# Moving four heads of an output projection from the 512-column pass to the 128-column tail of a decode attention kernel

## The chip, the core and the metric

The kernel runs on one core of a Trainium2 chip. The metric is device time in microseconds of one execution; the time before is the median of three runs.

## The reference, cut to what matters

For two batch rows of 512 values (`B, D = 2, 512`), with 32 query heads, 8 key and value heads, a cache of 32768 positions and heads of 128 values:

```python
xn = _layernorm(x, axis=-1)
q = (xn @ wq)                                # 32 heads of 128
scores = einsum("bhqd,bhkd->bhqk", q, k) * (Dh ** -0.5)
p = _softmax(scores, axis=-1)
o = einsum("bhqk,bhkd->bhqd", p, v)
s = o.reshape(B, Sq, Hq * Dh) @ wo           # (4096, 512)
h = relu(xn @ w1 + b1) ** 2
g = _silu(h @ w2 + b2)
return x + s * g
```

The caches are 512 MB of float32, read once. `wo` is 8 MB: 32 heads of 128x512 float32, 256 KB each.

## The kernel before, in words

One pair of batch row and key/value head is cut in two halves of 16384 positions, so there are `NT = 32` steps. In each, `kslot` receives 8 MB of keys and `vslot` 8 MB of values, both single buffers; TensorE multiplies the four queries of the group with the keys (`pe_scores`), a softmax piece is formed on VectorE and ScalarE, and TensorE multiplies the probabilities with the values (`pe_values`). Each engine runs its own loop; the order between them is set by semaphores alone. SP issues all large loads on one queue, each as soon as its buffer is free. Three prologue turns (`PRO = 3`) go through the same `pe_values` code with other contents in `vslot` and `pT`: the two matrices of the gate and `wq`.

`pe_values` (line 357) is 32 products. Product `n` takes 16 columns of `pT` as weights and 512 columns of `vslot` as the moving operand, and adds into `o_ps`, into the quarter of its partitions that `n % 4` names. Ahead of products 8, 16, 24 and 28 it waits for the semaphores `ge`, `gb`, `gc` and `gd`. In the loop these were given their counts beforehand, or are given them by loads.

After the 32 steps comes the product with `wo`, over the 32 heads of both rows, in three kinds:

- Heads 0 to 11 (`NX`, the first piece): their weights are in `wbuf`, their attention outputs in `oX`, and `pe_extra` (line 392) adds 12 wide products into `wb`.
- The further pieces of 8, 4 and 4 heads: SP loads them into `vslot` at places 8 to 15, 24 to 27 and 28 to 31 (semaphores `ge`, `gc`, `gd`), VectorE writes the heads' outputs to the same places of `pT` (`turned`, lines 405 and 406), and one more turn of `pe_values` adds them into `o_ps`. The other 16 places of `pT` are set to zero (line 407), so their products run over zeros.
- The last four heads (`TOP`), in pieces of 2, 1 and 1 (`TAIL`): their weights go to `wbuf` behind the first twelve, their outputs to `oN`. Each head takes four products (line 422), one for each block of 128 columns of `wo`, into the four quarters of partitions of `acc`. So `acc` holds 128 columns where `o_ps` holds 512.

The wide sums are brought to the shape of `acc` by a fold: VectorE adds `wb` and `o_ps` in two halves into `o_sb` (line 415; `t_w` names the two), and four products with the selection matrix `selg` (line 426) add the four blocks of 128 columns into `acc`. TensorE runs its instructions in program order, so the place of the fold among the narrow heads is written out: `if h == TOP - 2`, behind the third of four. Last, VectorE multiplies `acc` with the gate, adds `x`, and SP stores 64 KB (lines 430 to 434).

SP's last block (line 324) issues the loads of `wo`: the first at once, the piece of eight when product 15 of the last step is done (`vh`), all others when the last step's `pe_values` is done.

## Time and profile before

| | |
|---|---|
| runs before, median of 3 | 1302.14 us (1302.06 to 1302.2) |
| span of the profiled execution | 1300.8 us |
| its own time | not listed apart from the span; the median is 1.3 us above it |
| busy in the span: TensorE products, weight loads, VectorE, ScalarE, GpSimd | 53%, 15%, 7%, 8%, 0% |
| moved | 561 MB, 431 GB/s |

The profile is of one execution, times are from its start. A float32 product is two instructions (passes), each with its own weight load; products on different quarters of the partitions run beside each other, so several times of one instruction overlap. A busy share of TensorE is therefore no share of its peak. "PEld" is TensorE's weight load, "SPq" a transfer's issue by SP.

### The profile page before, as it was taken

What the parts mean: (1) busy time and instruction counts of PE and PEld (TensorE: products, weight loads), DVE (VectorE), ACT (ScalarE), POOL (GpSimd) and SP (SyncE); (2) the same over time, 40 slices, a digit from 0 to 9 for tenths busy, and PEclk for the clock granted to TensorE, in tenths of its full rate; (3) what the DMA queues carried; (4) which work ended last, traced back from release to release, by engine and by line L of the source; (5) the groups of instructions that cost most, each with busy time, mean ns of one, the idle gap of its engine ahead of it and who ended that gap; (6) DMA issues with size and microseconds to landing.
All of it is one profiled execution on the core that took longest, in us unless ns stands there. A gap on an engine that the chain in (4) does not pass through costs nothing.

```text
span 1300.8 us, 11201 instructions
## 1 busy us (share of the span) xinstructions
PE 691.4 (53%) x4781; PEld 189.5 (15%) x4781; DVE 86.0 (7%) x366; ACT 99.1 (8%) x202; POOL 5.7 (0%) x22
## 2 busy tenths in 40 slices
PE   3746546545545545645544644654554554554557
PEld 0111111111111111111111111111111111111112
DVE  2100000000000000000000000000000000000001
ACT  0301001010010001001010100001001000100100
POOL 1000000000000000000000000000000000000000
PEclk9877677677778677767767767767767767776878
DMA  9999999999999999999999999999999999999998
GB/s 420 419 451 419 447 423 429 441 419 451 419 451 419 451 419 431 439 419 451 419 451 419 451 419 431 439 419 451 419 451 419 451 419 431 439 419 451 419 435 373
DMA packets 10840, 561.08 MB, mean 431 GB/s; under 512 B 1216, under 2 KB 1368, under 8 KB 1752
## 3 DMA queue, kind: packets, MB, share of 16 engines
q1 hardware_dynamic: 10800, 561.06, 99.8%
q10 hardware_dynamic: 40, 0.02, 0.0%
HBM read 561.01 MB, written 0.07 MB: 431 GB/s over the span
## 4 chain that ended last, share of the span: by engine, by line
DMA 74%; PE 24%; issue 1%; DVE 0%; POOL 0%; SPq 0%; POOLq 0%
DMA vslot<-in_vt 70%; PE o_ps L364 24%; DMA wbuf<-in_wo 3%; DMA vslot<-in_wm 1%; PE wb L392 0%; DVE vslot L209 0%; DVE vslot L206 0%; PE acc L422 0%; POOL pT L197 0%; POOL pT L179 0%; SPq L243 0%; PE acc L426 0%; SPq L242 0%; DVE yb L430 0%; DVE xb L432 0%
## 5 line engine op out<-in xcount | busy, mean ns | idle before, releaser
L364 PE MATMUL o_ps<-vslot,pT 128*16 128x512 f32 x2304 | 327.6, 732 | 225.7 <-DMA vslot<-in_vt 201.5
L347 PE MATMUL sc<-kslot,qz 128*32 128x512 f32 x2048 | 294.1, 739 | 277.1 <-DMA kslot<-in_kt 277.1
L347 PEld LDWEIGHTS sc<-kslot,qz 128*32 128x32 f32 x2048 | 71.2, 132 | 478.5 <-DMA kslot<-in_kt 284.7
L364 PEld LDWEIGHTS o_ps<-vslot,pT 128*16 128x16 f32 x2304 | 69.6, 112 | 454.6 <-issue 223.5
L309 ACT ACTIVATE prob<-sc,nm 128x512 f32<-128x512 f32 x32 | 22.0, 687 | 633.9 <-DVE nm L277 633.9
L270 DVE TENSOR_REDUCE r<-sc 128x1 f32<-128x512 f32 x32 | 22.1, 692 | 557.7 <-PE sc L347 557.7
L318 ACT COPY o_sb<-o_ps 128x512 f32<-128x512 f32 x32 | 18.8, 586 | 480.2 <-PE o_ps L364 480.2
L353 PE MATMUL tp<-ident,prob 128*128 128x128 f32 x128 | 25.6, 333 | 50.7 <-ACT prob L309 50.7
L291 DVE TENSOR_REDUCE t<-ot 128x4 f32<-128x64 f32 x32 | 7.2, 225 | 547.6 <-PE ot L374 547.6
L374 PE MATMUL ot<-ident,o_sb 128*128 128x128 f32 x140 | 23.0, 287 | 25.0 <-ACT o_sb L318 22.9
L353 PEld LDWEIGHTS tp<-ident,prob 128*128 128x128 f32 x128 | 16.4, 164 | 56.8 <-ACT prob L309 56.8
L350 PE MATMUL ms<-ident,r 128*128 128x128 f32 x32 | 10.3, 323 | 26.4 <-DVE r L270 26.4
L374 PEld LDWEIGHTS ot<-ident,o_sb 128*128 128x128 f32 x140 | 14.7, 140 | 57.3 <-ACT o_sb L318 52.4
L311 ACT COPY pT<-tp 128x512 f32<-128x512 f32 x32 | 18.8, 586 | 28.4 <-PE tp L353 28.4
L309 ACT ACT_TABLE_LOAD x16 | 20.5, 1283 | 0.3
L350 PEld LDWEIGHTS ms<-ident,r 128*128 128x128 f32 x32 | 4.2, 133 | 55.4 <-DVE r L270 55.4
L355 PEld LDWEIGHTS ms<-selh,l 128*128 128x128 f32 x64 | 12.1, 236 | 0.0
L355 PE MATMUL ms<-selh,l 128*128 128x4 f32 x64 | 10.5, 235 | 0.0
L273 DVE TENSOR_REDUCE mh<-ms 128x4 f32<-128x128 f32 x32 | 9.3, 292 | 10.9 <-PE ms L350 10.9
L200 ACT COPY vslot<-wbuf 128x4096 f32<-128x4096 f32 x2 | 7.1, 3610 | 0.0
L309 ACT ACTIVATION_READ_ACCUMULATOR prob<-sc,nm 128x1 f32 x32 | 6.2, 192 | 0.0
L392 PE MATMUL wb<-wbuf,oX 128*16 128x512 f32 x24 | 4.4, 900 | 2.2 <-DMA wbuf<-in_wo 2.2
(86 smaller groups left out, 78.0 us busy)
## 6 DMA issues: line engine op xcount, KB each, us to landing
vslot<-in_vt SPq DMA_DIRECT2D x2, 4096.0 KB, 24.0
vslot<-in_wm SPq DMA_DIRECT2D x1, 7168.0 KB, 19.4
wbuf<-in_wo SPq DMA_DIRECT2D x1, 3072.0 KB, 34.9
vslot<-in_wo SPq DMA_DIRECT2D x1, 2048.0 KB, 13.6
vslot<-in_wo SPq DMA_DIRECT2D x2, 1024.0 KB, 12.0
kslot<-in_kt SPq DMA_DIRECT2D x32, 29.4
wbuf<-in_wo SPq DMA_DIRECT2D x1, 512.0 KB, 13.9
wbuf<-in_wo SPq DMA_DIRECT2D x2, 256.0 KB, 14.2
```

The source lines that it names most:

```text
L270: v.tensor_reduce(r1[:, :], sc[:, :], axis=AX.X, op=ALU.max).then_inc(dm, 1)
L273: did(f"mh{u}", v.tensor_reduce(mh[:, u, :], ms[:, :P].rearrange("p (a h) -> p h a", h=REP), axis=AX.X, op=ALU.max))
L291: did(f"t4{u}", v.tensor_reduce(t4[:, u, :], ot[:, :].rearrange("p (i y e) -> p e i y", i=4, y=NG)[:, :REP], axis=AX.XY, op=ALU.add))
L309: nc.scalar.activation(prob[:, :], sc[:, :], AF.Exp, bias=nm[:, u:u + 1], scale=SCALE, accum_out=l1[:, :]).then_inc(ex, 1)
L311: copy(pT[:, :], tp[:, :]).then_inc(gv, 1)
L318: copy(o_sb[:, :], o_ps[:, :]).then_inc(os, 1)
L347: ins = mm(sc[32 * c:32 * c + 32, :], qz[:, 28 - 4 * j:60 - 4 * j], kslot[:, lo:lo + W], start=(j == 0), stop=(j == NJ - 1))
L350: tr(ms[:, :P], r1[:, :].to_broadcast([P, P]), ident[:, :]).then_inc(pe.sem, 1)
L353: ins = tr(tp[:, k * P:(k + 1) * P], prob[:, k * P:(k + 1) * P], ident[:, :])
L355: mm(ms[:, :REP], l1[:, :].to_broadcast([P, P]), selh[:, :], start=True, stop=True).then_inc(pe.sem, 1)
L364: ins = mm(o_ps[32 * y:32 * y + 16, :], pT[:, 16 * n:16 * n + 16], vslot[:, n * W:(n + 1) * W], start=(n < NG), stop=(n >= 32 - NG))
L374: ins = tr(ot[:, lo:lo + P], o_sb[:, n * DH:(n + 1) * DH], ident[:, :])
```

## The change

`WIDE` becomes 24, so `TOP` becomes 8. The pieces of `wo` keep their sizes and order, 12, 8, 4, 4, 2, 1, 1, and the packed array is the same; the second piece of four now counts as the first of the tail. The first piece of four goes to places 28 to 31 of `vslot` (semaphore `gd`); places 24 to 27 get no load, their weights are set to zero by a memset, and `gc`'s count comes from VectorE. Eight heads are in `oN`, which has twice its size, and take narrow products. The fold is placed behind the first narrow piece, of four heads.

```diff
-WIDE = 28
+WIDE = 24
 TOP = 32 - WIDE
-PIECES = (12, 8, 4, 4)
-TAIL = (2, 1, 1)
+PIECES = (12, 8, 4)
+TAIL = (4, 2, 1, 1)
 NX = PIECES[0]
...
         h = load(vslot[:, 8 * W:], h, 8, ge)
         sp.wait(at(VD, NT - 1))
-        h = load(vslot[:, 24 * W:], h, 4, gc)
         h = load(vslot[:, 28 * W:], h, 4, gd)
         for n, sem in zip(TAIL, tail_sem):
             h = load(wbuf[:, (NX + h - WIDE) * D:], h, n, sem)
...
     turned(pv[:, 8:16, :], 3, 5).then_inc(gb, 16)
-    turned(pv[:, 24:32, :], 5, 7)
+    turned(pv[:, 28:32, :], 5, 6).then_inc(gc, 16)
+    v.memset(pv[:, 24:28, 0:B], 0.0)
     v.memset(pT[:, :].rearrange("p (a h z) -> p a h z", a=2, z=16)[:, :, 0:8, 0:B], 0.0).then_inc(gv, 17)
     oV = oN[:, :, :].rearrange("p r (b z) -> p r b z", b=B)[:, :, :, 0]
-    t_add = dve.done(v.tensor_copy(oV.rearrange("p r b -> p b r"), oS[:, 14:16, :]))
+    t_add = dve.done(turned(oV, 6, 8))
...
-            if h == TOP - 2:
+            if h == TAIL[0] - 1:
                 for c in range(NG):
                     pe.wait(t_w[c // 2])
                     mm(acc[32 * c:32 * c + 32, :P], selg[:, :], o_sb[:, c * P:(c + 1) * P], start=False, stop=False)
```

## Rows read from the trace of the kernel before

**Rows 1.** The page: its span, the load queue, the chain by engine.

```profile
span 1300.8 us, 11201 instructions
...
q1 hardware_dynamic: 10800, 561.06, 99.8%
...
DMA 74%; PE 24%; issue 1%; DVE 0%; POOL 0%; SPq 0%; POOLq 0%
```

**Rows 2.** The chain that ended last, its end: start us, us, what.

```profile
1249.99 0.62 issue
1250.61 34.92 DMA wbuf<-in_wo
...
1285.67 4.45 PE wb L392 x24
1290.11 6.87 PE o_ps L364 x64
1296.98 0.85 PE acc L422 x24
...
1298.58 0.02 issue
```

**Rows 3.** Timeline of SP: issues of `wo`; the last row merges two.

```profile
1282.33 0.43 SPq L326 DMA_DIRECT2D vslot<-in_wo  x1
1282.80 0.43 SPq L326 DMA_DIRECT2D wbuf<-in_wo  x1
...
1283.28 0.91 SPq L326 DMA_DIRECT2D wbuf<-in_wo  x2
```

**Rows 4.** DMA issues of small windows: size, us to landing; last the store.

```profile
vslot<-in_wo SPq DMA_DIRECT2D x1, 1024.0 KB, 13.1
wbuf<-in_wo SPq DMA_DIRECT2D x1, 512.0 KB, 13.9
...
wbuf<-in_wo SPq DMA_DIRECT2D x1, 256.0 KB, 14.2
...
out<-xb SPq DMA_DIRECT2D x1, 64.0 KB, 1.5
```

**Rows 5.** Timeline of weight loads, an early wide row and the end: idle before, releaser.

```profile
1290.36 0.12 PEld L364 LDWEIGHTS o_ps<-vslot,pT 128*16 128x16 f32 x4 [0.31 <-issue]
...
1295.51 0.12 PEld L364 LDWEIGHTS o_ps<-vslot,pT 128*16 128x16 f32 x4 [0.31 <-DMA vslot<-in_wo]
...
1296.78 0.41 PEld L422 LDWEIGHTS acc<-wbuf,oN 128*32 128x32 f32 x16 [0.72 <-issue]
1297.40 0.16 PEld L422 LDWEIGHTS acc<-wbuf,oN 128*32 128x32 f32 x8 [0.22 <-DMA wbuf<-in_wo]
...
1297.92 0.14 PEld L426 LDWEIGHTS acc<-o_sb,selg 128*32 128x32 f32 x4 [0.16 <-DVE o_sb L415]
```

**Rows 6.** Timeline of VectorE after the loop.

```profile
1284.64 0.09 DVE L407 MEMSET pT<- 128x32 f32 x1
...
1297.12 0.76 DVE L415 TENSOR_TENSOR o_sb<-o_ps,prob 128x256 f32<-128x256 f32 x2 [12.15 <-PE o_ps L364]
```

**Rows 7.** Timeline of TensorE: narrow products under way in two small windows.

```profile
1296.81 0.43 PE L422 MATMUL acc<-wbuf,oN 128*32 128x128 f32 x8
...
1296.81 0.54 PE L422 MATMUL acc<-wbuf,oN 128*32 128x128 f32 x12
```

**Rows 8.** Windows: busy us of PE, PEld, DVE, ACT, POOL, granted clock, DMA, GB/s.

```profile
1290.00:1299.00 9.00, 8.56 (x108) 2.82 (x100) 1.12 (x4) 0.59 (x1) 0.00 (x0) 1.00 0.82 330
```

**Rows 9.** Timeline of the start: a small load, GpSimd's last memset, their first users.

```profile
1.28 0.60 ACTq L126 DMA_DIRECT2D prob<-in_xr  x1
...
3.19 1.81 POOL L119 MEMSET vslot<- 128x2048 f32 x1
...
11.67 0.67 DVE L139 TENSOR_REDUCE st<-prob 2x1 f32<-2x512 f32 x1 [8.81 <-DMA prob<-in_xr]
...
17.30 0.17 DVE L165 COPY pT<-xs 128x8 f32<-128x8 f32 x1
```

## The prediction

> **What bounds the kernel now.** I began with the page. The one queue that carries all loads is busy 99.8% of the span, and the chain of work that ended last is three quarters DMA [rows 1]: for most of 1300.8 us the kernel is a stream of bytes, and what the engines do beside it is free. The change leaves every byte, every transfer and their order alone (below), so only the end of the run can move: from the landing of the first twelve heads of `wo` at 1285.53 on, the same chain in order of time is TensorE without a break, 4.45 us of line 392, 6.87 us of line 364, 1.60 us of lines 422 and 426, then two VectorE operations and the store [rows 2].

> Next I put the queue beside that chain. With the issue times [rows 3] and the times to landing [rows 4], the last loads of `wo` land at 1282.33 + 13.1 = 1295.4 (the second piece of four heads), 1282.80 + 13.9 = 1296.7 (two), and, the last row of issues being two of about 0.45 us, at about 1283.75 + 14.2 = 1297.95 (the last head); the one ahead of that is seen below, at 1297.4. The loads of weights show what TensorE waited for [rows 5]. Its wide pass takes four instructions every 0.43 us, and product 28, which needs the second piece of four, loads at 1295.51 behind the same 0.31 us of idle as the early row at 1290.36: the piece landed with 0.1 us to spare, no wait. The third narrow head waits 0.2 us for its transfer (1297.40). The second half of the fold waits for the VectorE sum and loads at 1297.92. VectorE has both sums ready at 1297.12 + 0.76 = 1297.88 [rows 6], so that load follows it by 0.04 us. This is the one wait that the end hangs on: behind it come half a fold, one head and the drain.

> **The change part by part.**

> *Transfers.* The pieces were 12, 8, 4, 4 and then 2, 1, 1; they are now 12, 8, 4 and then 4, 2, 1, 1. SP issues seven loads of the same sizes in the same order past the same two waits; one has another destination and semaphore. Cost 0, and the landings above stay. Only their users move: the first piece of four, ahead of the second on the queue, now feeds products 28 to 31, the second (1295.4) the first four narrow heads.

> *Wide pass.* The loop still has 32 products; heads' places 24 to 27 now run on weights set to zero, as 0 to 7 and 16 to 23 do already. Do such products cost less? The pass is 64 instructions in 6.87 us [rows 2], 0.107 us each, and the weight loads of a place over zeros (1290.36) stand at the same spacing as those of product 28 [rows 5]. So nothing is saved: the pass ends at 1296.98 as before. That product 28 has its data one piece earlier is worth 0 here, since it did not wait.

> *Four more narrow heads.* Each is four column blocks of two instructions. The eight in flight just before 1297.0 span 0.43 us, the twelve just after it 0.54 [rows 7]: four more instructions cost 0.11 us, so a head costs 0.213 us. The other bound is the chain's 0.85 us for the 24 instructions of three heads [rows 2], 0.283 us a head, which has the 0.2 us wait in it; a head is nearer to the first. [...]

> *The fold.* It moves from behind three narrow heads to behind four. Narrow work begins at 1296.81 [rows 7] in both kernels; four heads of 0.213 run until 1297.66, with no wait, their transfer having landed at 1295.4. The first half of the fold has its sum by 1297.50 (half of 0.76 behind 1297.12) and runs to about 1297.87; the second half still waits for 1297.88 and loads at 1297.92. So the extra head ahead of the fold is free: it fills the 0.2 us in which TensorE waited for the third head's transfer. If a head costs 0.283, four end at 1297.94 and the fold ends 0.2 us late.

> *Behind the fold* there are four heads where there was one: three more, 3 x 0.213 = 0.64 us. They end at 1298.15 + 4 x 0.213 = 1299.0, plus the drain of 0.2. Their transfers (landed at 1296.7, 1297.4, 1297.95) are needed from 1298.15, 1298.58 and 1298.79 on: the last has 0.8 us of slack.

> *VectorE, GpSimd.* A memset is added, of 128x8 where the one at 1284.64 writes 128x32 in 0.09 us [rows 6], and a copy has 128x16 elements in place of 128x8, among the same short operations. What waits for them on TensorE is line 392, held until 1285.5 by its transfer anyway, and the wide pass, behind it on TensorE; cost 0, covered by at least 0.8 us. If that cover were gone they would cost some 0.1 to 0.2 us, one or two such operations. At the start `oN` is twice as large: 128 more columns cost its memset about 0.11 us, a sixteenth of the 1.81 us that the padding of `vslot` (2048 columns) takes behind it. That padding is done at 5.0 us and first needed by an operation at 17.30 [rows 9]. Cost 0, with 12 us of cover.

> *Code.* TensorE's last straight stretch grows by 64 instructions (16 products, each two loads and two passes). Does fetching them cost? Entering the last stretch shows 0.72 us without loads where 0.31 is usual [rows 5], 0.41 us that nothing in the profile explains, yet the products of the narrow heads begin at 1296.81 [rows 7], while the wide pass by the chain still drains, to 1296.98 [rows 2]. SP's entry into its last block shows 0.62 us of issue, where ahead of line 430 there is 0.02 [rows 2]. I take 0 and keep a stall as a rival. [...]

> **Sum.** 0 (transfers) + 0 (wide pass) + 0 (head ahead of the fold) + 0.64 (three heads behind it) + 0 (the rest) = +0.64 us. The span of 1300.8 becomes 1301.4; the timed median is 1302.14, 1.3 us above the span for what lies around it, and I add to that: **1302.8 us**. The bounds of the head's cost give 3 x 0.213 = +0.64 to 3 x 0.283 + 0.2 = +1.05. A measurement of this kernel can tell about 0.2% from no change, here 2.6 us: so this is no change that can be measured.

> **The rivals.**

> *The landings decide instead (some gain).* The profile shows product 28 with only 0.1 us in hand and the last transfer with 0.8. If transfers land x later in the executions that are timed than in the one profiled, the kernel before loses almost all of x at product 28, the changed one only what exceeds 0.8. The difference is 0.64 - x, at best 0.2 us faster: 1301.9 to 1302.6. For it speaks how close the landing is; against it that the timed runs lie within 0.14 us.

> *A fetch stall in the longer last stretch (slower).* One stall, between the narrow heads. The prices: the 0.62 us of SP's entry; 1.5 us for the store of 64 KB, on a queue that is free by then [rows 4]; and for a small load under a full queue 10.4 us, from its issue at 1.28 to its first user at 11.67 [rows 9]. At 1297 the queue is nearly drained, so 1.5 is nearest: 0.64 + 1.5 = +2.1, 1304.3. It is slower by over 0.2% from a stall of 2.0 us on. Against it: the stretch as it is shows no gap there that a transfer or VectorE doesn't explain. [...]

> *The clock falls at the end (slower).* At half the clock eight heads cost 8 x 0.213 = 1.7 us more and the fold 0.4: +2.8, 1304.9. Against it: 1.00 was granted from 1290 to 1299 [rows 8], with TensorE busy 8.56 of these 9 us, and it stays busy.

> *The change does less than it says.* It shortens nothing: its wide pass keeps 32 products. That is in the forecast, not beside it.

> **How the numbers follow.** Forecast (+0.64 to +1.05): 0.75. Landings: 0.14. Fetch stall: 0.08, half of it over 2.0 us. Clock: 0.02. The remaining 0.01 is for a gain over 0.2%, for which I find no room: 2.6 us is more than the whole 1.6 us of narrow work and fold behind line 364. Faster 0.01, slower 0.04 + 0.02 = 0.06, same 0.93. The range takes in the landings' best case, 1301.9, the forecast, and the lower price of the fetch stall (0.64 + 0.62, on the forecast's upper bound 1303.8): 1301.9 to 1303.8; longer stalls and the clock, some 0.07, are left out.

> **What would show it.** In the changed kernel's trace: seven loads with landings as above; line 364 at 64 instructions with steady 0.43 us groups up to the end; 64 instructions of line 422, half ahead of the fold without a wait; the second half of the fold 0.04 us behind the second sum; and 2.2 us, not 1.6, from the end of line 364 to line 430. It is wrong if TensorE waits among the last heads for something that is neither a transfer nor VectorE, if the narrow heads behind the fold run slower than 0.11 us for four instructions, or if products over zeros turn out cheaper.

## The result and the profile after

The changed kernel takes 1305.56 us (median of 8 runs, 1304.74 to 1306.72), the kernel before 1302.11 us in the same runs; the ratio is 1.0026, 95% interval 1.0018 to 1.0035. It is slower by 3.45 us, where +0.64 was forecast and 1303.8 was the end of the range. The profiled execution took 1305.14 us, its span is 1303.7 us.

The changed kernel's chain that ended last, its end (start us, us, what); it answers to [rows 2]:

```profile
1290.60 5.34 PE o_ps L363 x48
1295.94 0.88 PE acc L422 x32
1296.82 0.38 PE acc L426 x6
1297.20 0.01 PE acc L422 x2
1297.21 0.10 PE acc L426 x2
1297.31 0.23 PE acc L422 x9
1297.53 3.02 issue
1300.55 0.88 PE acc L422 x21
1301.43 0.03 issue
```

TensorE stands still for 3.02 us among the heads behind the fold, and the chain finds nothing that it waited for: "issue". Without this piece line 430 would begin at 1301.45 - 3.02 = 1298.43 at the earliest, where it began at 1298.60 before; with the last head's weights landing only at 1298.2 (below) and the 0.5 us from such a landing to line 430 that b_half shows later, it would be about 1298.7. The weight loads of the same stretch say how far TensorE had come; they answer to [rows 5]:

```profile
1294.91 0.12 PEld L363 LDWEIGHTS o_ps<-vslot,pT 128*16 128x16 f32 x4 [0.31 <-issue]
1295.64 0.91 PEld L422 LDWEIGHTS acc<-wbuf,oN 128*32 128x32 f32 x32 [0.62 <-issue]
1296.56 0.44 PEld L426 LDWEIGHTS acc<-o_sb,selg 128*32 128x32 f32 x6
1296.90 0.11 PEld L422 LDWEIGHTS acc<-wbuf,oN 128*32 128x32 f32 x2
1296.92 0.12 PEld L426 LDWEIGHTS acc<-o_sb,selg 128*32 128x32 f32 x2
1296.93 0.33 PEld L422 LDWEIGHTS acc<-wbuf,oN 128*32 128x32 f32 x9
1300.55 0.58 PEld L422 LDWEIGHTS acc<-wbuf,oN 128*32 128x32 f32 x21 [3.29 <-issue]
```

Behind the fold 2 + 9 = 11 passes had run; 21 were left. So the stop lies inside a head, in the middle of products that share one transfer and one semaphore, at no wait of the program. Nor was a transfer late: the issues of the last four loads and the last ones' time to landing are

```profile
1283.25 1.86 SPq L326 DMA_DIRECT2D wbuf<-in_wo  x4
...
wbuf<-in_wo SPq DMA_DIRECT2D x1, 256.0 KB, 13.5
```

the last of the four being issued at about 1284.7 and landed at about 1298.2, 2.4 us before TensorE went on. What is new stands in the page's list of queues (queue: packets, MB, share), and a window of 0.5 us shows when it moved:

```profile
q1 hardware_dynamic: 10800, 561.06, 99.6%
q8 instruction: 1, 0.02, 0.0%
...
q8 instruction: 1, 0.02, 16.5%
```

The first two lines are the page's, the third is of the window 1297.5 to 1298.0. An instruction queue with one transfer of 0.02 MB, just behind the beginning of the stop; the page of before has no such queue.

### The profile page after: what moved, and what is told of

It reads as the page before. It is cut to its first block, busy times and chain, and to the rows that moved or that the text cites. A ratio compares the mean times of both kernels' runs of the same rounds, so it can differ in the third digit from the quotient of the medians.

```text
span 1303.7 us, 11266 instructions
## 1 busy us (share of the span) xinstructions
PE 699.0 (54%) x4813; PEld 194.0 (15%) x4813; DVE 85.9 (7%) x367; ACT 99.0 (8%) x202; POOL 5.8 (0%) x22
## 4 chain that ended last, share of the span: by engine, by line
DMA 72%; PE 26%; issue 1%; another core or an unknown queue 0%; DVE 0%; ACT 0%; POOL 0%; POOLq 0%
DMA kslot<-in_kt 70%; PE sc L346 23%; PE o_ps L363 2%; DMA vslot<-in_wm 2%; DMA vslot<-in_wo 1%; DVE vslot L206 0%; PE acc L422 0%; PE tp L352 0%; DVE r L270 0%; PE ot L373 0%; ACT o_sb L175 0%; ACT pT L311 0%; POOL pT L197 0%; POOL pT L179 0%
## 5 line engine op out<-in xcount | busy, mean ns | idle before, releaser
L346 PE MATMUL sc<-kslot,qz 128*32 128x512 f32 x2048 | 297.6, 746 | 275.9 <-DMA kslot<-in_kt 275.9
L309 ACT ACT_TABLE_LOAD x16 | 20.5, 1283 | 0.3
L313 ACT COPY lh<-ms 128x4 f32<-128x4 f32 x32 | 5.4, 168 | 0.0
## 6 DMA issues: line engine op xcount, KB each, us to landing
wbuf<-in_wo SPq DMA_DIRECT2D x1, 512.0 KB, 13.1
```

What stands on the lines that cost most here:

```text
L309: nc.scalar.activation(prob[:, :], sc[:, :], AF.Exp, bias=nm[:, u:u + 1], scale=SCALE, accum_out=l1[:, :]).then_inc(ex, 1)
L346: ins = mm(sc[32 * c:32 * c + 32, :], qz[:, 28 - 4 * j:60 - 4 * j], kslot[:, lo:lo + W], start=(j == 0), stop=(j == NJ - 1))
```

## The theories and the experiments

Theory F (fetch): TensorE's code reaches a block that is not loaded; the stop belongs to a place in the code, whatever is done there. Rival D (data): the heads behind the fold wait for a landing or for VectorE. Rival W (work): the narrow heads themselves are dear.

Places in TensorE's code are counted as follows: a float32 product is four instructions (the trace of before has 2304 weight loads and 2304 passes of line 364 for 36 turns of 32 products), a transpose two (140 weight loads and 140 passes of line 374 for 35 turns of four), and every branch, wait that stands alone, hint and register operation is taken as one, which is the author's assumption. The kernel before ends at place 426, the changed one at 490. The fold of the changed kernel ends at 426, and 22 instructions later, at place 448, it stood still (11 passes, each with its weight load). The padding of the experiments is repeated waits for a count of GpSimd that is long reached, at the start of TensorE's program, where it has nothing to do until 20.20 us; two such waits make one instruction (b_pad16 has 32 of them, and its page counts 11217 instructions, 16 more than before).

```diff
+    for _ in range(32):          # 16 instructions; 80, 16, 128, 308 for 40, 8, 64, 154
+        w(pool.sem, 1)
     nc.br("pe_values", engines=PE)
```

| run | kernel | code ends at | us, median (range) | profiled execution: time, span | stop |
|---|---|---|---|---|---|
| | before | 426 | 1302.1 | 1300.8 span | none |
| b_pad8 | before + 8 | 434 | 1302.12 (1301.89 to 1302.33) | 1302.24, 1300.9 | none |
| b_pad16 | before + 16 | 442 | 1305.73 (1305.44 to 1306.50) | 1305.67, 1300.8 | behind the span |
| b_pad40 | before + 40 | 466 | 1305.21 (1304.73 to 1305.66) | 1305.66, 1304.3 | 3.13 us |
| | changed | 490 | 1305.56 (1304.74 to 1306.72) | 1305.14, 1303.7 | 3.02 us |
| a_split | changed, branch added | 492 | 1305.84 (1304.77 to 1306.35) | 1305.42, 1304.0 | 3.29 us |
| a_hint | changed, branch and early hint | 493 | 1303.28 (1302.98 to 1303.45) | 1303.09, 1301.8 | none |
| a_hint_late | changed, branch and late hint | 493 | 1304.32 (1304.14 to 1304.71) | 1304.32, 1302.8 | 1.24 us |
| b_half | before, 16 score products out | 362 | 1302.10 (1301.98 to 1303.98) | 1302.10, 1300.8 | none |
| a_half | changed, 16 score products out | 426 | 1302.38 (1301.99 to 1304.55) | 1302.38, 1301.1 | none |
| a_half_pad64 | a_half + 64 | 490 | 1305.64 (1305.29 to 1306.63) | 1305.42, 1304.0 | 3.16 us |
| a_pad154 | changed + 154 | 644 | 1307.18 (1306.66 to 1308.91) | 1307.01, 1305.7 | 5.77 us |

**Moving the code of the kernel before.** For 16, 40 and 8 instructions:

> The kernel before with 16 more instructions (repeated waits that are long satisfied) at the start of TensorE's program, 20 us ahead of its first use, so every later instruction stands 16 places further back. Theory F (fetch): in the changed kernel TensorE stands still for 3.02 us at 1297.53, in front of the 448th instruction of the kernel's own TensorE code, because a block of code begins there; the code of before ends at place 426, so 16 more still fit: no stall, no transfer on the instruction queue, 1302.1 us (within 0.3). Rival D (data: a landing or VectorE): no effect of code length, 1302.1 too. Rival W (the narrow heads themselves are dear): 1302.1 too. This run is the control for the next.

> The same with 40 added instructions: the code ends at place 466, so its last 18 instructions lie beyond place 448. No transfer, no product and no wait of the end is changed. Theory F: a stall of 2.5 to 3.5 us inside the last narrow head (or the last product of the fold) at 1298, one transfer on the instruction queue, +2 to +4 us: 1304 to 1306. Rivals D and W: 1302.1, no stall.

> The kernel before with 8 added instructions, code end at place 434. With 16 the timed runs grew by 3.6 us though the span did not (1300.8), so there the block was missing for what TensorE still has to run behind the kernel's last instruction. Theory F: if that closing code is up to 14 instructions long, 1302.1; if it is 15 to 22, about 1305.7 with a span of 1300.8. Rivals D and W: 1302.1.

With 40 instructions the kernel before has the changed kernel's stop, with none of its changes. The chain of that run:

```profile
1296.90 1.01 PE acc L424 x24
1297.91 0.21 PE acc L428 x7
1298.12 3.13 issue
1301.25 0.42 PE acc L428
1301.67 0.44 PE acc L424 x8
```

Seven passes of the fold (line 428 here) are 14 instructions behind place 434: again place 448, now in the fold and not among the heads behind it. The ratio is 1.0023 (1.0014 to 1.0032). Rivals D and W fall with this run.

With 16 I was wrong: 1302.1 was expected, 1305.73 measured (ratio 1.0029, 1.0018 to 1.0039). Its page has the span of before and no instruction queue:

```profile
span 1300.8 us, 11217 instructions
...
q1 hardware_dynamic: 10800, 561.06, 99.8%
q10 hardware_dynamic: 40, 0.02, 0.0%
```

The same execution took 1305.67 us, 4.9 us more than its span; before and with 8 added instructions it is 1.3 us more. The whole loss lies behind the last instruction that the profile shows. What TensorE still runs there is not seen; that it needs 7 to 14 places, so that it fits behind 434 and not behind 442, is a reading that agrees with these runs and is not shown. All eight runs of this kernel have the gap, 4.8 to 5.4 us. The kernel before could have grown by 8 to 15 instructions, and not by more, without this loss.

**The block asked for ahead of time.** Three runs put the last two narrow heads in a section of their own; two of them add a branch hint, one instruction placed ahead of the branch to it. What the hint does is read from the runs. The cut shows a_hint:

```diff
     with nc.body("pe_extra", valid_engines=PE):
+        tail_hint = nc.tensor.mark_branch_hint_location()
...
+    with nc.body("pe_tail", valid_engines=PE):
+        w(dve.sem, n_dve + 2)
+        narrow(pieces[:2], 0)
+        nc.tensor.br("pe_last").branch_hint(tail_hint)
+    with nc.body("pe_last", valid_engines=PE):
+        narrow(pieces[2:], sum(TAIL[:2])).then_inc(pe.sem, 1)
+        nc.br("end", engines=PE)
```

`narrow` is the loop of the narrow heads with the fold as before; a_split is this without the hint, a_hint_late has the hint as the first instruction of `pe_tail`.

> The changed kernel, with its last two narrow heads in a code section of their own, entered by a branch for which a prefetch hint is given at the start of the section of line 392, some 14 us earlier. All work, transfers and waits stay. Theory F: the block is there in time, the 3.0 us stall goes, about 1302.3 (1301.8 to 1302.9). Rivals D and W: 1305.5 as the changed kernel, since data and work are the same.

> As the run before with the same branch, without the hint: the control for splitting the code. Theory F: the stall stays, 2.5 to 3.5 us, 1304.5 to 1306.5. If the branch alone removed it, the hint would have shown nothing. Rivals D and W: 1305.5.

> The changed kernel with the hint given at the start of the narrow heads (1296) instead of at line 392 (1283), for the same branch in front of the last two heads. Theory F with a fetch of about 3 us from the time it is asked for: TensorE reaches the end of its block 1.5 us later, so the stall is 1 to 2 us instead of 3, and the last landing is back at 14.2 us or less: 1303.3 to 1304.5. If the hint only starts the transfer when the branch is near, the stall stays whole: 1305.5. Rivals D and W: 1305.5.

Without the hint the stop stays (3.29 us, at the 11th pass again). With it the stop is gone, with data and work unchanged. But a_hint is at 1303.28, not 1302.3: the end now hangs on the last landing. Its chain, then the instruction transfer in the window 1292 to 1293, then its last two loads:

```profile
1283.78 15.25 DMA wbuf<-in_wo
1299.02 0.04 issue
1299.07 0.47 PE acc L392 x8
...
q1 hardware_dynamic: 58, 0.39, 94.2%
q8 instruction: 1, 0.02, 6.6%
...
wbuf<-in_wo SPq DMA_DIRECT2D x2, 256.0 KB, 15.2
```

6.6% of 16 engines' 1 us is 1.06 us of one engine for the block, between its share of the loads, and the last loads land 15.2 us after their issue, before 14.2 [rows 4]. The late hint is the trial of it: there the block moves at 1297.0, and the last two loads land 14.1 us after their issue, as was expected; in a_pad154 (below), whose block moves at 1286.4, among the loads, they take 15.5 us. How a block of 0.02 MB costs a landing 1 us stays argued, from the sizes agreeing. Of the stop the late hint leaves 1.24 us (the middle line is of the chain, the others of the timeline):

```profile
1296.20 0.14 PEld L392 LDWEIGHTS acc<-wbuf,oN 128*32 128x32 f32 x4 [0.30 <-issue]
...
1298.40 1.24 issue
...
1299.64 0.65 PEld L392 LDWEIGHTS acc<-wbuf,oN 128*32 128x32 f32 x21 [1.51 <-issue]
```

The hint stands ahead of the weight load at 1296.20, so TensorE went on some 3.4 us after it asked, about as long as its weight loads stand still without a hint (3.29 us in the changed kernel). The hint instruction moves the code by one place, and the stop comes one instruction earlier too: behind the 11th weight load and ahead of its pass, which is place 448 again.

**The change's own work, without the code.** Half of the score products of a step are left out in both kernels, so the scores of half the positions come out as zero; the loop stays bound by loads:

```diff
-        for j in range(NJ):
+        for j in range(4):
...
-start=(j == 0), stop=(j == NJ - 1)
+start=(j == 0), stop=(j == 3)
```

> The kernel before with 16 of its 32 score products per step left out (columns of the key half that the other 16 hold then count as zero scores, so the output is another one), which takes 64 instructions out of TensorE's code; the loop stays bound by the loads. The control for the next run. Theory F: the code ends at place 362, far from 448: 1302.1 (within 0.5), 1.3 us above its span. Rivals D and W: the same.

> The changed kernel with the same 16 score products left out: its code ends at place 426, as that of the kernel before, with all its own transfers, wide and narrow products and waits of the end. Theory F: no stall, no transfer on the instruction queue; what is left against the run before is the change's own work at the end: +0.64 us by my sum, or about -0.2 by the changed kernel's trace with its 3.02 us taken out (line 430 would stand at 1298.4 there, 1298.6 before). Rivals D and W: +3.4 us against the run before, 1305.5, since the end's data and work are those of the changed kernel.

> The run before with 64 repeated waits' worth of instructions put in front, so that its code has the length of the changed kernel's again. Theory F: the stall is back, +2.5 to +3.7 us against the run before, at the 11th pass behind the fold. Rivals D and W: as the run before.

The pair differs by 0.28 us (1302.38 and 1302.10; spans 1301.1 and 1300.8); their intervals against the kernel before, 0.9996 to 1.0014 and 0.9994 to 1.0012, overlap almost wholly, so the runs can't tell this difference from none. With the code back at the changed kernel's length the time is back: +3.26 us against a_half, 3.16 us of stop in the profile. The two parts, 0.28 + 3.26 = 3.54, come close to the 3.45 that the change cost.

The chain of a_half at the end:

```profile
1289.72 6.87 PE o_ps L363 x64
1296.58 0.87 PE acc L422 x32
1297.46 0.36 PE acc L426 x6
...
1297.93 0.90 PE acc L422 x30
1298.83 0.02 issue
```

From the end of the wide pass to line 430 it takes 2.27 us. In b_half the weight loads show why the kernel before gains less from its shorter tail than its own chain said:

```profile
1294.77 0.13 PEld L364 LDWEIGHTS o_ps<-vslot,pT 128*16 128x16 f32 x4 [0.30 <-issue]
1295.50 0.26 PEld L364 LDWEIGHTS o_ps<-vslot,pT 128*16 128x16 f32 x8 [0.60 <-DMA vslot<-in_wo]
...
1298.07 0.16 PEld L422 LDWEIGHTS acc<-wbuf,oN 128*32 128x32 f32 x8 [0.25 <-DMA wbuf<-in_wo]
```

There product 28 waits for its transfer, and the last head for its own: the wide pass is early, the landings are not. The same holds with all work of the kernel before: in b_pad16 product 28 and the last head (0.24 us) wait for their transfers, and the multiplication with the gate begins at 1298.53, where line 430 began at 1298.60.

**The stop moved to a place where TensorE waits anyway.**

> The changed kernel, all work kept, with 154 added instructions at the start of TensorE's program: place 448 now falls on the first instructions of the section of line 392 (place 447 on), which TensorE enters at about 1283 and where it then waits some 2.5 us for the first twelve heads. Theory F: the fetch of 3 us is paid there, where TensorE has this wait and 0.3 to 1.2 us more ahead of product 8; no stall in the narrow heads. What is left: the 16 KB on one of the 16 DMA engines among the loads; in the run with the hint that transfer took 1.06 us of one engine and the last landing was 15.2 instead of 14.2 us after its issue. So 1302.4 if this delay is hidden, up to 1303.5 if it carries through. Rival D/W: 1305.5, data and work being those of the changed kernel. If two blocks are not kept beside the new one, the return to the wide pass stalls once more: 1305 to 1309.

A miss. The stop did move there, but was 5.77 us long, not 3:

```profile
1282.47 0.66 PE ot L375 x4
1283.13 5.77 issue
1288.90 0.37 PE ms L389
1289.28 5.04 PE wb L393 x24
...
q1 hardware_dynamic: 23, 0.38, 88.5%
q8 instruction: 1, 0.02, 6.6%
```

(The last two lines are of the window 1286 to 1287.) The weight load of line 389, place 448, had run at 1282.99, and its pass, place 449, is the first thing behind the stop. The stop ends 3.5 us behind the landing that line 393 needs (issued at 1249.58, landed 35.8 us later), and nothing behind makes that up. In the four runs with a whole stop in the narrow part (the changed kernel, b_pad40, a_split, a_half_pad64) it lasts 3.0 to 3.3 us, with the loads nearly drained; here, with the load queue full, almost twice that. The difference lies ahead of the block's transfer, not in it: by windows of 0.1 us the transfer begins 3.3 us behind the start of the stop here and 0.4 to 0.6 us behind it in those four, and from its beginning to TensorE going on it takes 2.5 us here and 2.5 to 2.9 us there. There was no second stop on the way back to the wide pass.

No kernel here beats the one before: the change without the stop, a_half against b_half, is no gain.

## Why the prediction was wrong, point by point

- *Transfers, wide pass, clock:* right as to the terms. Seven loads of the same sizes; line 363 with 64 instructions, products over zeros no cheaper (6.87 us in a_half, 6.87 before); the granted clock was 1.00 through the narrow heads. That the pass ends at 1296.98 as before did not hold: it ended at 1295.94. The prediction looked at the clock from 1290 on only. Before, line 392 had run at a mean granted clock of 0.62 (0.50 from 1286.5 to 1288.5) and took 4.45 us; in the changed kernel it had 1.00 and took 2.77 us, and product 8 then waited for its transfer until 1290.60. The change need not be the reason: b_pad16, the kernel before with padding, took 2.77 us as well, behind the same 2.2 us without products as before, and a_hint_late, the changed kernel with a branch and a hint, took 4.46 us behind the same 2.2.
- *Code:* this step failed. "I take 0 and keep a stall as a rival": the 64 added instructions crossed place 448, and the block behind it was not there: a stop of 3.02 us. That the stretch of before "shows no gap there that a transfer or VectorE doesn't explain" was no evidence: it ended before the block did, and what runs behind the span was not in view. I saw that the code grew and did not count where it stood. The 0 for the added instructions was the author's estimate, made beside the 0.41 us at the entry into the last stretch; no row showed a block reached in straight code. How long a block is was not shown either: the runs met one boundary, at place 448.
- *The price of the rival* was off as well: 1.5 us from the store was the row I called nearest; it is 3.0 to 3.3 us with the queue nearly drained and 5.8 us with it full. No run shows that such a stall costs what a store does; taking the store's price was the author's estimate, and the changed kernel had one transfer of 0.02 MB on the instruction queue and a stop of 3.02 us in its place. The forecast of that rival, 1304.3, and its condition (over 2.0 us is a measurable loss) were of the right kind; its chance, 0.08, was not.
- *Three heads behind the fold,* +0.64: right as to the path (2.27 us from the end of the wide pass to line 430 in a_half, 2.2 forecast, 1.6 before), mis-sized as to the total, +0.28. The sum started both kernels from the same end of the wide pass. In b_half the wide pass has to wait at product 28, and the last head for its weights, and in a_half neither does. So the rival of the landings took back about half of the term, as far as these two traces go; the timed difference of 0.28 us is within the runs' spread.
- *Head ahead of the fold, VectorE, GpSimd:* 0, as forecast.

## What to carry to other kernels

Count the instructions of an engine ahead of the kernel's last stretch, and find by padding how far the next code block is: here it began at place 448, a block that was first reached in the last stretch cost 3.0 to 3.3 us on the path, and 40 harmless instructions at the start of TensorE's program were enough to reach it (b_pad40). "Issue" in the chain (3.02 us in the changed kernel) beside a transfer on an instruction queue was its mark; a timed run that grew (by 3.6 us in b_pad16) while the span did not was, by the reading above, its mark behind the span. Moving code by padding told such a loss from a loss of work in one run (b_pad40).
